# A smaller inverse for the first two steps, a's products on GpSimd, and a rewritten order in a chunked recurrence with soft routing

## The chip, the cores and the metric

One core of a Trainium2 chip. The time is device microseconds of one execution; the median of three runs of the kernel before is 380.5 us.

## The reference

For each of 4 batches and 8 heads (32 pairs) a 40x40 state runs over 768 steps of time. At each step the output row is `r_t @ state`, and then

```
Sa    = state @ a_t
state = state * w_t - outer(Sa, b_t) + outer(v_t, k_t)
```

The 32 outputs are joined into x, 3072 rows of 320. A soft mixture of 8 experts follows: `logits = x @ phi` (32 slots), a softmax over the rows sends rows to slots, each expert (320 to 1024, relu, back to 320) works on its 4 slots, and a softmax over the slots brings the results back to the 3072 rows.

## The kernel before, in words

**Chunks.** Time is cut into 12 steps (`st`, NST) of C = 64 positions, each of two halves (`q`) of 32; two steps make a super-step (`ss`). Inside a half the recurrence is a triangular system: with L the strictly lower part of b's products with a, u = (1 + L)^-1 g has to be found for each of the 32 pairs.

**Preparation of a step**, on data alone: `scan_s`, `scan_k` and `scan_c` (lines 758 to 807) make the running products of w by scans on VectorE (DVE), multiply k and b by one of them and a by the other; `bda_at` spreads a into a block-diagonal tile with ScalarE (ACT); `gram` and `lgram` multiply them on TensorE (PE) and mask them with DVE; `kbtok` and `ctok_of` transpose them. From step 2 on the scans stand in PSUM, in two halves of six groups.

**The solver** (lines 905 to 922) inverts the 32x32 triangles of a whole super-step at once: `solve_in` transposes on DVE and copies on ACT, then `solve_step(ss, i)` for i = 1 to 30 issues two instructions on GpSimd (POOL), a product of i x (31 - i) elements for each of 128 partitions and its addition, each needing the one before it; `solve_out` transposes back on DVE.

**The chain** of a step: `chain_g(st, q)` gathers g with products of the state and v, `chain_u(st, q)` (line 955) multiplies it by the inverse with 32 small products and copies it out negated, for q = 0 and then 1; `chain_s` (line 974) makes the next state. `y_vut`, `y_sd`, `y_p`, `y_y` compute the outputs of the step before; `slots_*` collect the routing every second step. Step st of the chain runs beside the preparation of steps st + 3 and st + 4, the outputs of step st - 1 and half of a later super-step's solver (`sol`, lines 1296 to 1303).

**The tail** (lines 1317 to 1405): the last outputs and the routing, the first expert layer, then for each half of the 320 output columns (`hf`) 64 products of the second layer into `so`, a sum, and 24 products of 160 columns that are copied out of PSUM two at a time and stored in runs given by `OX`.

**What sets the order.** Every call on `nc` is recorded by `Plan.record` (line 236) as an operation; successive products of one shape into one bank are joined into one. `Plan.schedule` (line 375) reads the order in which operations are placed from the string `ORDER`, two characters an operation; `forward` (line 383) estimates times, chooses PSUM banks, keeps POOL and DVE operations apart where both read SBUF (`clash`), and lets DMA issues on SyncE (SP) wait for PE work (`LAG`, `SLOTS`). `fill` puts products that compute nothing into estimated gaps of PE. All engines therefore run a fixed sequence each:

```
self.order = [self.ops[at[2 * i] * len(CODE) + at[2 * i + 1]] for i in range(len(self.ops))]
```

Of the kernel before, what the change touches and what calls it, by code (L numbers as in the profile page):

```python
# [116 lines left out]
class Engine:  # L117
# [35 lines left out]
    r"$w&/%f%g&<&=&?&@&A&B&(&R&S&T&U&[&]&`%{&a&e&f&g&h&k&l&9&s&t&u&v&w&x&y%)%s':%Z'3&8&z&{&|'$'%'i&O'j'q'r's&3't'u'v'w'x"
    r"(#'''+%~($%|(%',(&%[&2('(($,(.&0&K&:&1&5&*&J(/%]&4&;&+&,&p%^%b&%&-%a&m&F$-%h(6(7&$&q%z'&&)'1%i&>%3%j&E%k'2&&%l'/%m"
    r"%K&r%V$p&N'*&G&n%W%q%L%M%4&}'>&'%X'0&D%J%N'#$q'(&H&I&L&C&~(8&o'-%Y(Z%d%t%x%w'?%u%-%v'F%.'='`%e&6'@(c&7&V(9'B&X&Y&Z"
    r"'A'{'_&W&^'.';(<(0&i&c&_&j(1'4'|'9'<&d'C'}&M'a'D'U'6'5'G'7(2'H'I'J'K'Z']'X(='b'L'8(U'O'E'~'P'^'R(q'S(R(3'Y'Q'T'M(@"
    r"'c'd'f(j'e'V'y'W(4(S)&'N'[()(-(,(>([(?'g(A'z'm'k(+(5'n(*'l(B'o(G(Q(T(V(k'p(r(L(H(`(W(J(P(I(e(l)'(s(z({(C(d(O(|).(D"
    r'(i(K)0(E(a(M(b(g)*(y)((N(})1)/)+)])^+)+*+1)_+2+3+4+5+6+7+8+<+=+>+?+@+A+B+C+F+G+L+M))+N+O+P+Q+R+S+T+U+V+W+X+Y+`+a+h'
    r"+i+j+k+p+q+r+s+v+w(f)V(Y(v)z(X&Q);'h(:)@(w(t(;):)A)h(u(x%p),(o+x)=)2(^(m(h)-)3)B+y)<(F)C(p(~+z(n)>(_)4+{)i)|)R)S)H"
    r"(])?*.)P)T)5)D)j)Q)I)#)8)6)$)7)m)9)E)X)L)U*$){*'+|*6)Y)n)J)F)M)r)K*/*<*P*7)s+})%)G)e)`)k)f)c)d)Z)N*))a)b*2*%*3*H*8"  # L160
    r'*+)g)O*,*=*9)o***1)l*>*-,$*a*V*?)p*Q)[)t)W*E)q)u)w)v,%,&)y*z*W*@)~,O*L*y*4)x*^*F*[*i*R*A*]+I*B*#*_*&*:*C*M*`*N*S*h'
    r"*;*w+e*0*I*j)},@+H*k*O+K*x,'*b*J*(*c*o##,(+J*p+b*g*f+c+f%o+++~*d*e,G+%+E,3+g+&*D*K*T*5*U+d+#+$*q,>+,,R+(*r+-*s,P,^"
    r"-w+',W,C+.,#*u*t,k,l*v,X+Z+[,o+],Q,A,m,E+t+^,)+D,?+_+/-3+0,=+u-4,-,n*X,L,4,.,I*Y,p,U,_,a,`,B,5,/-Q,6,M,J,S,N,b,u,w"
    r',T,K,y,<,x,s,7,v,j,f,D-g,z,H,t,*-I-J,+,q.s-C-F.t.{.|.}.~/#/$/%/&-(/*-R-:/+/,,F/-/.///0/1/4/5/:/;/</=/>/?/@/A/B/C/D'
    r"/E/F/G-K/M,r,{%n,c,V/N/U/V/W/X-+,d-E-9-5-'-G-6-H-,-T/^,,/_/`/a/d/e/f,g,h,e,i,|,Y-Y,[,}.#-S,]0>-1-2.$-/,Z-0-D-<---Z"
    r'-*,~-=-;-.-i-U-?-@->.9-x-A/g-%-&-#-W-V-d.5-_-$-r-f-X.:*l-z-B-~.;.<*G-)/O.e-`-m*m-o-p/h-e.d/i-s/j-7/k/n-8-n*Z*n*{.%'
    r'.2-L-y.)-{-h-l-M-P.3.1.A.8*|-O/o.C+l-N-t.B-[-u/p*}-v-]/P.D-a.&*~.*.,.+.-.6.7-^-b-c.J-|.H.U.=+m...p./.o.K.L+n.>-k/Q'
    r'.?.@-j.0.I.f/R+9.T-}00.M.g.N.O.[+:.^.Q.P-q.R.`/q.u.S/r.m.n._.a.q.v0.,0/S/7,1.].V/H.w0E.W.y.x0B/60O/206.z.r/s.E/J/l'
    r"0L0-/K/I/L/t/80,/~03.'.b/90+/T.c0P/u0b0T.F+o/m+;0X/v0c180#.(0D19012b2c2j2k1f2l2m2n2o2p2q2u2v2w2x2y2z2{2|3#3$3)3*3+"
    r'3,3-3.3/30313233343536,83<3=3D3E3F0/0s0U0r0M020N0$0V090A0%0;/w/b07/33G3L0&3M3N3O3R0W/x0C0<0f0t0:3S0g0h0i0z0=0Y0@0x'  # L170
    r'/y0v/c0?3T0y0^0_0Q0w1$0`0R0j0u0S1%0|1H3U040a0d05120{0Z3V1#0}0[1C0]0~0k1(1X1D1Z0e.X.41U0l1).G1I.Y1+0m.Z1w0o1*3W100p'
    r".h0n1.1,0q1t1x1@1/.i1&1A083X3Y3]111'150H1g141l1Y1T0I.j1M1-/Y1_1S.k0J1F3^17161W1]1G0K/Z1R1;2'1?1=1<1|1V1>/[1E.l201N"
    r"210F1i1J1`/'1r2(3_1B0G1K1h1a22131L2)1c/(1d1O3`1s1^2R1b2$232%241u1e3%1:1P2*2&2C3&1j1Q2S1v2}2,2-2D1y1z251{2N2E2.2+1k"
    r"29273'3(2/3a2O3b2L2F3A2>2:2M282A2^2@2B1p3>1}3B2?1[2<1~/]3?2=3C,2/{2T2[2_2#/z3w2U3z2]44/|3x262`2h2i3v373c3:5=573~4@"
    r"4<3;384A4o1n392G1o0'2H4p5|3d5}6(6)6*3@6+6,6-6.6/636465666768696:6=6>6?6@6A6B6C6D6E6F6G6H6I6J6K6L2P6R6S6T1m6U6V3o3{"
    r'1q3}2;/)2a2~6W754*3p6]3f2I2J4+4,2d3y4%0(3|2K3g3h4&2f6^4=3q6_472e6`4P4>2Q6c452V2g4Q4?464$2W494:4F4D6d3e4R2X3P4S,92Y'
    r"4H6e6f4'6g6h4X4;4#482Z4V4K3Q4Y4-4B4W4L5B4I2r4G4Z4E3j4J5D4O4T4c4N5,4M4e4U4l6i745(5.5/4]4f4i5*3H4C4d3m4[4y5'5+5E3I4k"
    r'4^4j4r3n4s4m3J2s4v4n7<5)4g4t4w4u6j6k6l7=4{424h545$4x5R6m4_4.5A4|4}555%5&5c565U504z4/525J6;4~5S0)5Z5T5O4q535#4`5P5K'
    r"5V434a5Q4b3K4(5L4)5j5e5^5k6<6n5W5i5g5o5f5h5[5C5`5q5z5-7&5?,:5{3i6o5]5l/}7(5H5a5_7'5d5@5M6p3k5u5I5v5w5x6q5N6X6Y5X2t"
    r',;407)6M415m5b5y6P6N6Q5p5n51597D6Z6O5s7B5t7+6{7A5r7@5Y6|717*6}6t727.7J6&7k6u5>7/6$5~6v6#7C7-737P7N7F7G7S6%7,7a7K7I'  # L180
    r"7Q7H7L6r3Z6s7E7T7U7O7?7Z7X7R6a77703[7Y0*7]7_7W7M5:7g7{8,6'8&7e7^8$7b7z877:6x8%7l7}7|7V9)7c7h62607~8#3r587d8/7`3l6["
    r"7m7i7n7o7q7p8'808)7j7[8*7f8-7w888D7x8.7y6~7t848+7r618?8A857u7v818E8@868283988C8:7s6b8{8(7>8|8K5F8T3s8B8;898<8=8L8F"
    r'8z8`8N8H7#767$8J8a8I8^8G9<8R8U7%8P8_5;8[91938>9%789&6w7;8S8]8g8M968Q8h3t3u8i9?5G8k8j8V94959=6y8~8l8b9C8W8}8X8Y9D8O'
    r"9#8Z9'9E8m9A9>9$8n9I5<8p8d9(9F9h90979B8e998o8v9@9X9J9G9O8c9S8q9T8w9K9Q9^9`9R9Y9_9b9P9a9c9f9d8x9q799e9U9L9k9{9V6z9M"
    r'9Z9r9x8y:N9N9s9[9W9y9z9|9t9]9}8f9-9i8s9~9:9+9u:#9/:$9v:+:%9m8r8u:&9n9l:1:,:-:3:2:.:59g8t:/:0:4:7:8:692:I:9:::;9o9w'
    r":':<:=9p:?:>:A9,:@:B:O9H:_9j:P:C:`:Q:a:D:R9.:S:E:(:U:X:h:T:V:Y:F:]:i:G:b:W:^:c:):J:[:K:m:Z:M:j:l:k:d:g:e:f9;;7;8:*"
    r":L:H:n9*;9:r;:;;:s:o:p;C:t;D:q;A;R;B:u;E;P:v;>;H;Q;-;S;T;F;U;V:y;0:~;W;G;I;&;.;?;#;';J;1:w;+;$:x:{;%;<:|;K;(;=;X;4"
    r';);5;@;M;2;*;Y:z;3:};L;Z;N;,;/;6;O'
# [1280 lines left out]
```

## Time and profile before

| | |
|---|---|
| median of three runs | 380.5 us (379.73 to 381.6) |
| the profiled execution's own time | 377.92 us |
| its span, first to last instruction | 376.1 us |
| mean granted clock of TensorE | 0.941 |
| busy in the span: PE, DVE, POOL, ACT | 90%, 71%, 52%, 44% |
| moved by DMA | 63.05 MB, 168 GB/s on average |

All operations are issued from one place, so the profile gives them one line, L1223; the products that compute nothing have L479, and a stretch counted for L1223 alone leaves them out. Operations are told apart by engine, shape and tile: `wt` stands for the eight large tiles, in which most buffers lie, `mem`, `old` and `mid` for others, `ps` for the banks of PSUM, `cs_t` for the constants. A product in fp32 is seen as two records, each with a weight load (PEld). [...]

### The profile page before, as it was taken

The numbers are of one execution on the slowest core, as the hardware profiler recorded it, in microseconds if no ns is written. First come the engines' busy times: TensorE is split into PE (matmuls) and PEld (weight loads), VectorE is DVE, ScalarE is ACT, GpSimd is POOL, SyncE is SP. The second block draws the span as 40 slices with busy tenths as digits, with TensorE's granted clock in tenths as the row PEclk, the third lists the DMA queues.
The fourth block names the chain that finished last, engine by engine and source line by source line (L and its number), as shares of the span: only waits on it lengthen the run. The fifth ranks groups of instructions, "written<-read, shape, count | busy, mean of one in ns | idle before, by whom it ended". The sixth has DMA issues, their size and how long they took to land.

```text
span 376.1 us, 18254 instructions
## 1 busy us (share of the span) xinstructions
PE 337.4 (90%) x7957; PEld 291.6 (78%) x7957; DVE 267.0 (71%) x603; ACT 166.6 (44%) x377; POOL 195.0 (52%) x381
## 2 busy tenths in 40 slices
PE   8594888999999979899999998998999798999991
PEld 8592676888898969778898887998797687863791
DVE  5578896888989878878899797955476354573242
ACT  0543836535465452752745735352533223440331
POOL 3358888888688802888268870888600000020000
PEclk9966776999999998999999999999999889999996
DMA  7975674216645473433463535457486928799528
GB/s 190 244 185 142 163 184 131 68 34 159 160 134 170 122 172 88 132 86 82 104 192 93 163 83 170 141 151 215 119 240 189 290 74 250 199 345 416 205 99 321
DMA packets 35368, 63.05 MB, mean 168 GB/s; under 512 B 5001, under 2 KB 22521, under 8 KB 35289
## 3 DMA queue, kind: packets, MB, share of 16 engines
q1 hardware_dynamic: 35289, 61.89, 56.9%
...
q14 instruction: 17, 0.14, 0.1%
HBM read 57.94 MB, written 3.93 MB: 165 GB/s over the span
## 4 chain that ended last, share of the span: by engine, by line
PE 73%; DMA 7%; DVE 5%; ACT 5%; issue 4%; POOL 3%; SPq 1%; DVEq 0%; ACTq 0%
PE ps L1223 73%; DVE wt L1223 4%; ACT wt L1223 4%; POOL wt L1223 3%; DMA wt<-in_rr_dram 2%; DMA mem<-in_rr_dram 2%; DMA wt<-in_w_dram 1%; DMA wt<-in_kb_dram 1%; DMA wt<-in_ww_dram 1%; SPq L1223 1%; ACT L1223 0%; ACT mem L1223 0%; DVE mem L1223 0%; DVE ps L1223 0%; ACT ps L1223 0%
## 5 line engine op out<-in xcount | busy, mean ns | idle before, releaser
L1223 PE MATMUL ps<-wt,wt 128*64 128x40 f32 (+9 forms) x3432 | 144.0, 240 | 7.9 <-issue 6.2
L1223 PEld LDWEIGHTS ps<-wt,wt 120*32 120x32 f32 (+7 forms) x3432 | 128.3, 130 | 18.0 <-issue 10.9
L1223 POOL TENSOR_TENSOR wt<-wt 128x58 f32<-128x58 f32 (+14 forms) x180 | 90.3, 502 | 38.9 <-ACT wt L1223 25.3
L1223 POOL TENSOR_TENSOR wt<-wt,wt 128x58 f32<-128x58 f32 (+15 forms) x183 | 95.3, 521 | 27.7 <-ACT wt L1223 12.5
L1223 DVE TENSOR_TENSOR wt<-ps,cs_t 128x384 f32<-128x384 f32 (+6 forms) x132 | 62.8, 496 | 27.0 <-PE ps L1223 24.4
L1223 PE MATMUL ps<-cs_t,wt 120*128 120x120 f32 (+5 forms) x496 | 64.3, 267 | 8.7 <-DVE wt L1223 3.1
L1223 PE MATMUL ps<-wt,mem 120*64 120x192 f32 (+4 forms) x880 | 60.0, 311 | 8.2 <-ACT wt L1223 4.5
L1223 ACT COPY wt<-ps 128x320 f32<-128x320 f32 (+2 forms) x92 | 42.3, 474 | 51.8 <-PE ps L1223 42.8
L1223 PEld LDWEIGHTS ps<-cs_t,wt 120*128 120x128 f32 (+5 forms) x496 | 48.2, 144 | 19.0 <-ACT wt L1223 4.7
L1223 PEld LDWEIGHTS ps<-wt,mem 120*64 120x64 f32 (+4 forms) x880 | 47.5, 131 | 13.3 <-POOL mem L1223 4.7
L1223 ACT COPY mem<-ps 120x256 f32<-120x256 f32 (+6 forms) x99 | 37.4, 402 | 41.7 <-PE ps L1223 39.5
L1223 DVE TENSOR_TENSOR_SCAN ps<-ps,wt 120x390 f32<-120x390 f32 x40 | 38.6, 967 | 2.6 <-ACT old L1223 1.3
L1223 DVE TENSOR_SCALAR wt<-ps 32x320 f32<-32x320 f32 x48 | 23.7, 493 | 18.8 <-PE ps L1223 18.0
L1223 DVE TENSOR_TENSOR wt<-wt,ps 120x384 f32<-120x384 f32 (+1 forms) x80 | 34.1, 447 | 2.5 <-DMA wt<-in_kb_dram 2.0
L1223 POOL MEMSET mem<- 128x2048 f32 x1 | 1.8, 1807 | 62.2 <-PE ps L1223 62.2
L1223 PE MATMUL ps<-mem 32*32 32x40 f32 (+2 forms) x776 | 32.2, 224 | 0.8 <-DMA mem<-in_rr_dram 0.8
L1223 ACT ACTIVATE wt<-wt,bm_t 120x768 f32<-120x768 f32 (+1 forms) x36 | 30.0, 863 | 2.7 <-PE ps L1223 2.6
L1223 ACT ACTIVATE wt<-ps 32x320 f32<-32x320 f32 x48 | 20.5, 426 | 21.9 <-PE ps L1223 20.3
L1223 DVE STREAM_TRANSPOSE wt<-wt 128x1024 f32<-128x1024 f32 x12 | 25.1, 2095 | 0.2
L1223 PEld LDWEIGHTS ps<-mem 32*32 32x32 f32 (+2 forms) x776 | 19.8, 117 | 5.1 <-issue 1.2
L1223 DVE TENSOR_TENSOR ps<-ps,wt 120x480 f32<-120x480 f32 (+1 forms) x30 | 17.5, 600 | 6.7 <-PE ps L1223 6.5
L1223 PE MATMUL ps<-wt 32*32 32x40 f32 x1536 | 19.3, 199 | 2.7 <-issue 2.2
...
## 6 DMA issues: line engine op xcount, KB each, us to landing
...
wt<-in_rr_dram SPq DMA_DIRECT2D x96, 40.0 KB
...
```

Of the source, the lines that this page charges most:

```text
L1223: nc.vector.memset(ex, 0.0)
```

## The change

Five things, and a new `ORDER` for the 2222 operations that there are then (2240 before):

- The solver of super-step 0 inverts only the two 16x16 diagonal blocks of each triangle: 14 steps in place of 30, each over both blocks (`halves`). `lgram` of steps 0 and 1 writes the diagonal blocks and, with a second mask, the off-diagonal block (`nn`). `chain_u` of steps 0 and 1 multiplies g by the block inverse, copies (ACT), multiplies by the off-diagonal block, adds to g (DVE), and then goes on as before.
- From step 4 on a's product is one GpSimd instruction of 768 elements on the copy `cp`, in place of two on DVE; for steps 2 and 3 it stays on DVE.
- In the scans of steps 2 to 11, w is copied into both PSUM tiles, the scan runs in place and gives the whole product at once, so that the small product for `pc` becomes a copy on ACT; k's and b's product is issued once for each half of the groups in place of twice.
- Loads of w1 for the two large row blocks are split in two by columns, 32 in place of 16.
- In the tail the second layer's products are recorded in four parts for each half, and results leave PSUM three at a time; the second half is stored in five runs in place of seven.

```diff
-KV = 3
-BM, AV = NST, 2
-OX = ((6, 12, 18, 24), (4, 8, 12, 16, 20, 22, 24))
+PA = 4
+BM = NST
+OX = ((6, 12, 18, 24), (6, 12, 18, 21, 24))
...
 ORDER = (
...
-    cs_t = cst.tile([128, 451], F32, name="cs_t")
+    cs_t = cst.tile([128, 515], F32, name="cs_t")
+    mask_d, mask_n = cs_t[:, 451:483], cs_t[:, 483:515]
...
-                nc.sync.dma_start(wv[:, 2 * p + k], w1[2 * i + p, 128 * k:128 * k + 128])
+                for f in (0, 512):
+                    nc.sync.dma_start(wv[:, 2 * p + k, f:f + 512], w1[2 * i + p, 128 * k:128 * k + 128, f:f + 512])
...
+        nn, ys = cht(mid[:, 4 * HD:4 * HD + 1024]), mid[:, 0:HD]
...
         def scan_s(st):
-            if st > 1:
-                w_t, pc = raws[st], pcs.put(st)
-                sbk[st] = [[bank(f"s{k}{st}{x}")[0:120, 0:6 * CP + 2] for k in "kc"] for x in range(2)]
-                for x, (t, u) in enumerate(sbk[st]):
-                    a, g = 6 * CP * x, slice(6 * x, 6 * x + 6)
-                    t = t[:, 0:6 * CP]
-                    nc.scalar.copy(u, w_t[:, a:a + 6 * CP + 2])
-                    nc.vector.tensor_tensor_scan(
-                        t[:, ::-1], u[:, 2:6 * CP + 2][:, ::-1], one_f[:, a:a + 6 * CP][:, ::-1], 0.0, ALU.mult, ALU.add)
-                    nc.vector.tensor_tensor(pc[:, g], gcp(w_t[:, 0:NG * CP])[:, g, 1], gcp(t)[:, :, 0], ALU.mult)
-                    nc.vector.reciprocal(gcp(inj_f[:, a:a + 6 * CP])[:, :, 0], pc[:, g])
+            w_t, pc = raws[st], pcs.put(st)
...
+            sbk[st] = [[bank(f"s{k}{st}{x}")[0:120, 0:6 * CP] for k in "kc"] for x in range(2)]
+            for x, (t, u) in enumerate(sbk[st]):
+                a, g = 6 * CP * x, slice(6 * x, 6 * x + 6)
+                nc.scalar.copy(t, w_t[:, a + 1:a + 6 * CP + 1])
+                nc.vector.tensor_tensor_scan(
+                    t[:, ::-1], t[:, ::-1], one_f[:, a:a + 6 * CP][:, ::-1], 0.0, ALU.mult, ALU.add)
+                nc.vector.reciprocal(gcp(inj_f[:, a:a + 6 * CP])[:, :, 0], gcp(t)[:, :, 0])
+                nc.scalar.copy(pc[:, g], gcp(t)[:, :, 0])
+                nc.scalar.copy(u, w_t[:, a:a + 6 * CP])
         def scan_k(st):
-            if st > 1:
-                k_t = kbt(st)
-                for x, (t, _) in enumerate(sbk[st]):
-                    g, s_v = slice(6 * x, 6 * x + 6), gcp(t[:, 0:6 * CP])[:, :, 0:C].rearrange("p g (q t) -> p g q t", q=2)
-                    for q in range(2):
-                        nc.vector.tensor_tensor(k_t[:, g, :, q], k_t[:, g, :, q], s_v[:, :, q].unsqueeze(2).broadcast_to([120, 6, 2, 32]), ALU.mult)
+            k_t = kbt(st)
...
+            for x, (t, _) in enumerate(sbk[st]):
+                g = slice(6 * x, 6 * x + 6)
+                kv = k_t[:, g].rearrange("p g k q t -> p g k (q t)")
+                nc.vector.tensor_tensor(kv, kv, gcp(t)[:, :, 1:CP].unsqueeze(2).broadcast_to([120, 6, 2, C]), ALU.mult)
         def scan_c(st):
-            ah = ahs[st]
-            if st > 1:
-                cp = gc(cps.put(st))
-                for x in range(2):
-                    a, g, t = 6 * CP * x, slice(6 * x, 6 * x + 6), sbk[st][x][1][:, 0:6 * CP]
-                    nc.vector.tensor_tensor_scan(t, t, inj_f[:, a:a + 6 * CP], 0.0, ALU.mult, ALU.add)
+            ah, cp = ahs[st], gc(cps.put(st))
...
+            for x, (_, t) in enumerate(sbk[st]):
+                a, g = 6 * CP * x, slice(6 * x, 6 * x + 6)
+                nc.vector.tensor_tensor_scan(t, t, inj_f[:, a:a + 6 * CP], 0.0, ALU.mult, ALU.add)
+                nc.scalar.copy(cp[:, g], gcp(t)[:, :, 0:C])
+                if st < PA:
-                    nc.scalar.copy(cp[:, g], gcp(t)[:, :, 0:C])
-                return
...
+            if st >= PA:
+                nc.gpsimd.tensor_tensor(ah, ah, cp, ALU.mult)
         def bd_load(key, bd, src):
...
-                nc.vector.tensor_tensor(
-                    lls[ss][:, 2 * p:2 * p + 2].rearrange("p q h t -> p (q h) t"),
-                    lps[st].rearrange("p (x t) -> p x t", t=32),
-                    mask_l.unsqueeze(1).broadcast_to([128, 16, 32]), ALU.mult)
+                for t, mask in ((lls[ss], mask_d if ss == 0 else mask_l), (nn, mask_n))[:2 if ss == 0 else 1]:
+                    nc.vector.tensor_tensor(
+                        t[:, 2 * p:2 * p + 2].rearrange("p q h t -> p (q h) t"),
+                        lps[st].rearrange("p (x t) -> p x t", t=32),
+                        mask.unsqueeze(1).broadcast_to([128, 16, 32]), ALU.mult)
         def solve_in(ss):
...
+        def halves(t, r, c, m):
+            ap = [list(t.ap[0]), [528, 2], [32 if r is None else 0, c[1] if r is not None else c[0]], [1 if c[2] else 0, m]]
+            return bass.AP(tensor=t.tensor, offset=t.offset + (0 if r is None else 32 * r) + c[3], ap=ap)
         def solve_step(ss, i):
+            if ss == 0:
+                m = 15 - i
+                tv = tmp_r[i % 4][:, 0:2 * i * m].rearrange("p (k j t) -> p k j t", k=2, j=i)
+                nc.gpsimd.tensor_tensor(tv, halves(n_t, None, (i, 0, 0, i), m), halves(lt, i, (0, i, 1, i + 1), m), ALU.mult)
+                nv = halves(n_t, None, (i, 0, 1, i + 1), m)
+                nc.gpsimd.tensor_tensor(nv, nv, tv, ALU.add)
+                return
...
         def chain_u(st, q):
+            if st < 2:
+                for x, (l, r_) in enumerate(((tt, gs), (nn, ys))):
+                    yp = bank(f"y{x}s{st}")
+                    for h in range(H):
+                        for b in range(B):
+                            r = slice(32 * b, 32 * b + 32)
+                            nc.tensor.matmul(yp[r, h * D:(h + 1) * D], l[r, c, h, :], r_[r, h * D:(h + 1) * D], start=True, stop=True)
+                    if x == 0:
+                        nc.scalar.copy(ys, yp[:, 0:HD])
+                    else:
+                        nc.vector.tensor_tensor(gs, yp[:, 0:HD], gs, ALU.add)
...
         def solve_items(ss):
-                    + [lambda i=i: solve_step(ss, i) for i in range(1, 31)] + [lambda: solve_out(ss)])
+                    + [lambda i=i: solve_step(ss, i) for i in range(1, 31 if ss else 15)] + [lambda: solve_out(ss)])
         def y_lists(st, w):
...
+            nc.tag = x // 4
+        nc.tag = ""
...
-        for r in range(0, 24, 2):
+        for r in range(0, 24, 3):
-            for x in range(2):
+            for x in range(3):
-            (nc.vector.tensor_copy if r % 4 else nc.scalar.copy)(wts[hf][:, HC * r:HC * r + 2 * HC], op[:, 0:2 * HC])
-            if r + 2 in OX[hf]:
-                nc.sync.dma_start(out[hf, :, HC * at:HC * (r + 2)], wts[hf][:, HC * at:HC * (r + 2)])
-                at = r + 2
+            (nc.vector.tensor_copy if r % 2 else nc.scalar.copy)(wts[hf][:, HC * r:HC * r + 3 * HC], op[:, 0:3 * HC])
+            if r + 3 in OX[hf]:
+                nc.sync.dma_start(out[hf, :, HC * at:HC * (r + 3)], wts[hf][:, HC * at:HC * (r + 3)])
+                at = r + 3
...
+    dg = np.kron(np.eye(2, dtype=f4), np.ones((16, 16), f4))
-                             np.concatenate([st] * 4)],
+                             np.concatenate([st] * 4), -np.tile(st * dg, (4, 1)), -np.tile(st * (1 - dg), (4, 1))],
```

## Rows read from the trace of the kernel before

**Rows 1.** The page, busy time, share of the span and instructions of each engine

```profile
PE 337.4 (90%) x7957; PEld 291.6 (78%) x7957; DVE 267.0 (71%) x603; ACT 166.6 (44%) x377; POOL 195.0 (52%) x381
```

**Rows 2.** Timeline of POOL: start, length, merged instructions, wait ahead and its releaser

```profile
26.14 33.65 POOL L1223 TENSOR_TENSOR wt<-wt,wt 128x30 f32<-128x30 f32 x57 [1.89 <-ACT wt L1223]
...
60.80 30.43 POOL L1223 TENSOR_TENSOR wt<-wt 128x30 f32<-128x30 f32 x50
...
147.15 19.98 POOL L1223 TENSOR_TENSOR wt<-wt 128x30 f32<-128x30 f32 x34 [14.74 <-ACT wt L1223]
```

**Rows 3.** Timeline around the first product with the first inverse

```profile
62.14 0.55 DVE L1223 TENSOR_TENSOR wt<-ps,cs_t 96x384 f32<-96x384 f32 x1 [2.92 <-PE ps L1223]
...
63.08 2.00 DVE L1223 STREAM_TRANSPOSE wt<-wt 128x1024 f32<-128x1024 f32 x1
...
65.13 0.79 PE L1223 MATMUL ps<-wt 32*32 32x40 f32 x64
...
66.07 1.00 DVE L1223 TENSOR_SCALAR wt<-ps 32x320 f32<-32x320 f32 x2 [0.42 <-PE ps L1223]
```

**Rows 4.** Stretches: length, PE, PEld, DVE, ACT, POOL busy, clock, DMA share, GB/s

```profile
40.00:65.10 25.10, 19.48 (x312) 15.96 (x311) 20.24 (x42) 14.03 (x28) 21.73 (x47) 0.76 0.59 160
...
52.00:62.00 10.00, 9.13 (x59) 7.45 (x60) 6.60 (x17) 4.04 (x10) 8.51 (x23) 0.50 0.51 142
...
65.10:340.30 275.20, 261.00 (x6905) 228.90 (x6905) 208.27 (x475) 128.33 (x300) 150.43 (x300) 0.98 0.55 155
...
368.00:376.10 8.10, 0.00 (x0) 0.00 (x0) 1.48 (x4) 0.75 (x2) 0.00 (x0) 0.58 0.82 320
```

**Rows 5.** The same shape on PE at two clocks, timeline

```profile
59.53 1.59 PE L1223 MATMUL ps<-wt,wt 120*96 120x96 f32 x8
...
79.83 0.92 PE L1223 MATMUL ps<-wt,wt 120*96 120x96 f32 x8
```

**Rows 6.** Groups by shape, POOL: busy us, mean ns, idle ahead

```profile
L1223 POOL TENSOR_TENSOR wt<-wt,wt 128x30 f32<-128x30 f32 x12 | 3.0, 247 | 13.1 <-ACT wt L1223 12.5
...
L1223 POOL TENSOR_TENSOR wt<-wt,wt 128x240 f32<-128x240 f32 x12 | 7.7, 645 | 0.9
...
L1223 POOL TENSOR_TENSOR wt<-wt,wt 120x768 f32<-120x768 f32 x3 | 5.1, 1699 | 1.7 <-DMA wt<-in_aa_dram 1.7
```

**Rows 7.** Groups by shape, PE, ACT and DVE

```profile
L1223 PE MATMUL ps<-wt 32*32 32x40 f32 x1536 | 19.3, 199 | 2.7 <-issue 2.2 <-ACT wt L1223 0.5
...
L1223 ACT COPY wt<-ps 128x320 f32<-128x320 f32 x48 | 19.9, 428 | 39.5 <-PE ps L1223 38.2 <-issue 1.2
...
L1223 DVE SCALAR_TENSOR_TENSOR slx<-slx,mem,ps 128x320 f32<-128x320 f32 x5 | 2.7, 541 | 1.5 <-PE ps L1223 1.5
...
L1223 DVE TENSOR_TENSOR wt<-ps,cs_t 128x512 f32<-128x512 f32 x12 | 8.3, 688 | 3.6 <-PE ps L1223 3.6
...
L1223 DVE TENSOR_TENSOR wt<-wt,ps 120x384 f32<-120x384 f32 x60 | 31.5, 543 | 2.2 <-DMA wt<-in_kb_dram 2.0
...
L1223 ACT COPY ps<-wt 120x392 f32<-120x392 f32 x20 | 9.8, 491 | 6.6 <-DMA wt<-in_ww_dram 4.3 <-DVE wt L1223 2.2
```

**Rows 8.** Waits of the DMA queue on SP: us in total, times, longest

```profile
SPq L1223 <- PE ps L1223: 198.1, 129, 8.9
```

**Rows 9.** Timeline of the last 25 us

```profile
356.83 4.55 PE L1223 MATMUL ps<-wt,mem 128*32 128x160 f32 x126 [0.38 <-DMA wt<-in_w_dram]
...
363.31 8.68 SPq L1223 DMA_DIRECT2D out_dram<-wt  x11
...
367.40 2.08 DVE L1223 COPY wt<-ps 128x320 f32<-128x320 f32 x5 [0.79 <-PE ps L1223]
```

**Rows 10.** Timeline where the second inverse is done and first used

```profile
94.38 2.09 DVE L1223 STREAM_TRANSPOSE wt<-wt 128x1024 f32<-128x1024 f32 x1
...
103.17 0.79 PE L1223 MATMUL ps<-wt 32*32 32x40 f32 x64
```

More of the change, by code (lines that the diff above doesn't have):

```diff
@@ L153 @@
[L153 to L162, printed above, removed]
@@ L740, in rwkv_softmoe @@
         s0_t = kbks.tiles[3][0:120, 0:NG * CP]
-        scans = Ring([(kbks.tiles[2][0:120, 0:NG * CP], inj_f)])
+        s1_t = kbks.tiles[2][0:120, 0:NG * CP]
         bbs = [t.rearrange("p (g q t) -> p g q t", q=2, t=32) for t in (so_f[:, 2 * NG * C:3 * NG * C], rts.tiles[0].rearrange("p g c -> p (g c)"))]
@@ L772, in scan_s @@
-            w_t, s_t = raws[st], s0_t if st == 0 else scans.put(st)[0]
-            nc.vector.tensor_tensor_scan(
-                s_t[:, ::-1], w_t[:, 2:NG * CP + 2][:, ::-1], one_f[:, ::-1], 0.0, ALU.mult, ALU.add)
-            pc = pcs.put(st)
-            nc.vector.tensor_tensor(pc, gcp(w_t[:, 0:NG * CP])[:, :, 1], gcp(s_t)[:, :, 0], ALU.mult)
-            nc.vector.reciprocal(gcp(inj_f)[:, :, 0], pc)
-        def scan_k(st):
-            if st > 1:
-                k_t = kbt(st)
-                for x, (t, _) in enumerate(sbk[st]):
-                    g, s_v = slice(6 * x, 6 * x + 6), gcp(t[:, 0:6 * CP])[:, :, 0:C].rearrange("p g (q t) -> p g q t", q=2)
-                    for q in range(2):
-                        nc.vector.tensor_tensor(k_t[:, g, :, q], k_t[:, g, :, q], s_v[:, :, q].unsqueeze(2).broadcast_to([120, 6, 2, 32]), ALU.mult)
-                return
-            k_t, s_t = kbt(st), s0_t if st == 0 else scans[st][0]
-            for q in range(2):
-                eng = nc.vector if st < KV and q == 0 else nc.gpsimd
-                eng.tensor_tensor(
-                    k_t[:, :, :, q], k_t[:, :, :, q],
-                    gcp(s_t)[:, :, 32 * q:32 * q + 32].unsqueeze(2).broadcast_to([120, NG, 2, 32]), ALU.mult)
@@ new lines, in scan_k @@
+        def scan_k(st):
+            k_t = kbt(st)
+            if st < 2:
+                for q in range(2):
+                    eng = nc.vector if q == 0 else nc.gpsimd
+                    s_v = gcp((s0_t, s1_t)[st])[:, :, 32 * q + 1:32 * q + 33]
+                    eng.tensor_tensor(k_t[:, :, :, q], k_t[:, :, :, q], s_v.unsqueeze(2).broadcast_to([120, NG, 2, 32]), ALU.mult)
+                return
+            for x, (t, _) in enumerate(sbk[st]):
+                g = slice(6 * x, 6 * x + 6)
+                kv = k_t[:, g].rearrange("p g k q t -> p g k (q t)")
+                nc.vector.tensor_tensor(kv, kv, gcp(t)[:, :, 1:CP].unsqueeze(2).broadcast_to([120, 6, 2, C]), ALU.mult)
@@ new lines, in scan_c @@
+        def scan_c(st):
+            ah, cp = ahs[st], gc(cps.put(st))
+            if st < 2:
+                ct = raws[st][:, 0:NG * CP]
+                nc.vector.tensor_tensor_scan(ct, ct, inj_f, 0.0, ALU.mult, ALU.add)
+                nc.vector.tensor_tensor(ah, ah, gcp(ct)[:, :, 0:C], ALU.mult)
+                nc.scalar.copy(cp, gcp(ct)[:, :, 0:C])
+                return
[4 more added lines that the diff above has]
+                if st < PA:
+                    nc.vector.tensor_tensor(ah[:, g], ah[:, g], gcp(t)[:, :, 0:C], ALU.mult)
+            if st >= PA:
+                nc.gpsimd.tensor_tensor(ah, ah, cp, ALU.mult)
```

86 lines of the change are left out of this document (50 added, 36 removed).

## The prediction

> **What bounds the kernel now.** The page comes first: TensorE is busy for 337.4 us of 376.1, no other engine for more than 71% [rows 1]. That is a mean, so the stretches come next, without the products that compute nothing. From 65.1 to 340.3 us PE has 261.0 us of work in 275.2, with the clock at 0.98: 14.2 us are idle, in many small pieces, and DVE with 208.3 is second [rows 4]. There a chain that comes earlier gains only where PE has gaps. From 40.0 to 65.1 it is another kernel: PE has work for 19.5 of 25.1 us at a mean clock of 0.76, and POOL is the engine that is nearly full, 21.7 us. The timeline of POOL says why: the first solver runs from 26.14 without a break, 57 instructions to 59.8, its last three behind the start of the second solver, which goes on at 60.80 [rows 2]. Then the inverse is transposed at 63.08, 2.2 us late, because DVE had an operation in front that waited 2.92 us for PE, and the first `chain_u` starts at 65.13, 0.05 us after the transposition [rows 3]. So the start is bound by POOL's solver, and the rest by PE.
>
> **The solver.** By size an instruction goes from 0.247 us at 30 elements to 0.645 at 240, which is 0.190 us and 1.895 ns an element [rows 6]. Before: 60 instructions with 2 x 4960 elements, 11.4 + 18.8 = 30.2 us; from 26.14 to the last at about 60.8 it took 34.7, so 0.07 us lie between two. After: 28 instructions with 2 x 1120 elements, 5.3 + 4.2 + 28 x 0.07 = 11.5 us. The access runs over one more dimension; no row prices that, and between nothing and a tenth more I take nothing. The inverse is there at 37.6 in place of 60.8, 23.2 us earlier; with the transposition's 2.1 us, and no operation in front of it, `chain_u` can start at about 40, 25 us earlier.
>
> **The two sets more.** Four calls of `chain_u` (steps 0 and 1, two halves) get two sets of 32 products, 0.79 us a set (the shape takes 19.3 us for 24 sets) [rows 3, 7]: 8 x 0.79 = 6.3 us more PE work. On the chain each call gets 2 x 0.79, an ACT copy of 0.43, a DVE addition of 128x320 at 0.54 (nearest row, the one that also scales) [rows 7], and four handovers of 0.05 to 0.15 [rows 3]: 2.9 us, 11.7 in all. If nothing but the chain counted, 25 - 11.7 = 13.3 us would be left. Queued behind the wait for the copies are PE's products in its fixed order, so the order has to put other products there. The second mask for steps 0 and 1 is 2 x 0.69 on DVE [rows 7], and stands behind the solver's input, not in front.
>
> **What PE can take back.** The earlier chain must find room on PE. Between 40.0 and 65.1 there are 25.1 - 19.5 = 5.6 us of idle. From 52 to 62 the clock stands at 0.50, with 9.1 us busy [rows 4]; the same eight products take 1.59 us there and 0.92 at 79.83 [rows 5], so that at the full clock 9.1 would be 5.3, 3.8 less. A PE that is kept busy from 40 on can win 5.6 + 3.8 = 9.4, of which the new sets take 6.3: 3.1 are left. The ends are 13.3 (chain alone) and -6.3 (nothing won back); I take 3.1, as from 65.1 on PE is at 95% and whatever is brought forward was work to be done anyway.
>
> **a's products.** DVE loses 8 x 2 x 0.525 = 8.4 us (31.5 us for 60) [rows 7], POOL gets 8 x 1.70 = 13.6 [rows 6]. [...] But neither engine is the path: POOL works for 150.4 of the 275.2 us [rows 4], and the solver of a later super-step begins after a wait of 14.74 us for its input [rows 2]. Two products for each super-step, 3.4 us, are hidden in such gaps; without that cover they would delay an inverse by 3.4. I take 0 on POOL.
>
> **The scans.** ACT gets 20 copies more at 0.49, 9.8 us [rows 7], and 20 small ones that no row shows, between nothing and 0.43 each. It has 128.3 of 275.2 us busy, and the copies serve steps that are three or four ahead: 0; without that cover some 2 x 0.5 us stand ahead of a step's a product. DVE loses the small products and half the issues of k's products; less load there shortens waits of PE, and an order that keeps the gaps smaller can also avoid a clock drop like the one above. I take 1.5 of the 14.2 idle us back, between -2 (the new order meets other stalls) and 5.
>
> **Loads and tail.** The w1 split adds 16 issues, which at the 0.79 us an output issue takes (8.68 us for 11) [rows 9] is at most 12.6 us of SP's queue. SP waits 198.1 us for PE's pace [rows 8], so 0; uncovered, a late w1 piece would hold the first expert layer by one issue. The constants grow by 64 columns, 32 KB, 0.1 us at the 320 GB/s of the end [rows 4]. At the end, the first stored half of the output is held until the second layer's last products, 356.83 to 361.38; the stores are issued from 363.31, the last copy ends at 369.48, and the queues work on to about 375 [rows 4, 9]. The products in four parts let one half's results go out between the other half's products: 3.93 MB at 320 GB/s are 12.3 us, so stores from 357.5 could end at 370, 6 us earlier; PE's own work there stays the same, and the half that is last has to follow it by its copies and half of the bytes. Between 0 and 6 I take 2.
>
> **The sum.** 377.9 (the profiled execution's own time) - 3.1 - 1.5 - 2.0 = 371.3. The median of the runs stands 2.6 above that execution, so 374 is predicted for the median. A measurement of this kernel can tell about 0.5% from no change, 378.6 to 382.4.
>
> **Rivals.**
> *The chain passes in full.* If PE's busy time has slack inside, the whole 13.3 us comes through, with the other terms 380.5 - 13.3 - 3.5 = 363.7, 364. For it speaks that weight loads are busy for 78% only, against 90% [rows 1]; against it, that a set of 64 records takes 0.79 us wherever it stands [rows 3, 10]. [...] Chance 0.17.
> *DVE takes the place of POOL.* From 40.0 to 65.1 DVE is busy for 20.2 of 25.1 us [rows 4]. The free 4.9 lose 1.4 + 4 x 0.54 = 3.5 to the new masks and additions, so only 1.4 us of the chain's own work can come forward, and preparation is pushed back as far as the chain comes earlier. Then 6.3 are paid, 1.4 + 3.5 won: 381.9, no change. Chance 0.14.
> *The second inverse is late: slower.* Step 2 can't start without it. Before, the second solver started at 60.80, its result was transposed at 94.38, and step 2 took it at 103.17 [rows 2, 10]. With two a products in between it now needs 34.7 + 3.4 + 2.1 = 40.2 us from its start, and step 2 is due at 103.2 - 3.1 = 100.1, so it decides if it starts after 60. It can, if the chain's DVE work goes ahead of the preparation of step 3, whose b products it inverts. A start at 70 costs 10 us of a waiting PE: 384. For it speaks DVE's load above; against it, that POOL is now free from 37.6 on, so the order has 22 us to spare for it. Chance 0.11.
>
> **How the numbers follow.** The forecast has 0.58; its own range is 369 to 378.5 from the tail's and the scans' ends. The likeliest time is 374. The range goes down to 364 for the first rival and up to 382 for the second; the third and the ends of the tails beyond are left out. Faster by over 0.5%: 0.58 + 0.17 = 0.75; no change 0.14; slower 0.11.
>
> **What would show it.** Right: POOL's first solver with 28 instructions in some 11.5 us; a first `chain_u` near 40 with sets of 0.79 between copies; the next stretches with PE above 90% and the clock at 1.00 before 60; stores that start before the second layer's last products are done. The forecast is wrong if step 2's first use of its inverse (103.17) comes over 8 us earlier (first rival), less than 1 us earlier or later (second), or right behind a transposition that ends after 101 (third).

## The result and the profile after

The changed kernel is slower: 383.4 us (median of 20) against 378.3 for the kernel before, a ratio of 1.013 with a 95% interval of 1.009 to 1.017, where 374.0 and a gain had been predicted. Executions of one kernel differ: the twenty of the kernel before run from 373.2 to 389.9 us, and compared with itself in the same way it gave 0.989 (0.979 to 0.998). A difference of 1% between two comparisons of a few executions proves little here, and the 0.5% of the prediction was too fine a measure. Medians below are over all executions of a comparison, while ratios with an interval leave out executions over 1.5% above the quickest of their kernel, so that the two need not agree.

The page of the changed kernel, from an execution of 383.19 us (span 381.4), engines and the two instruction queues [rows 1]:

```profile
PE 345.6 (91%) x8507; PEld 295.9 (78%) x8507; DVE 261.0 (68%) x547; ACT 177.5 (47%) x419; POOL 188.3 (49%) x357
...
q8 instruction: 67, 1.10, 1.2%
q14 instruction: 16, 0.13, 0.1%
```

Timeline of POOL, the first solver and the start of the second [rows 2]; it holds the 28 instructions forecast:

```profile
28.52 8.66 POOL L724 TENSOR_TENSOR wt<-wt,wt 128x28 f32<-128x28 f32 x20 [3.54 <-ACT wt L724]
37.24 0.15 POOL L724 MEMSET wt<- 128x32 f32 x1
37.32 2.96 POOL L724 TENSOR_TENSOR wt<-wt,wt 128x88 f32<-128x88 f32 x8
49.54 0.55 POOL L724 TENSOR_TENSOR wt<-wt 128x30 f32<-128x30 f32 x2 [9.26 <-ACT wt L724]
```

The solver takes 11.8 us and is done at 40.28. But the timelines of DVE and PE show the transposition of the inverse at 51.76 and the first extra set at 53.93 [rows 3]; the set on `mid` is the second, 57.05 is u, and 105.46 is step 2's first use of its own inverse [rows 10]:

```profile
46.31 2.07 DVE L724 STREAM_TRANSPOSE wt<-wt 128x1024 f32<-128x1024 f32 x1
...
49.39 0.98 DVE L724 TENSOR_TENSOR_SCAN ps<-ps,wt 120x390 f32<-120x390 f32 x1
...
51.76 2.02 DVE L724 STREAM_TRANSPOSE wt<-wt 128x1024 f32<-128x1024 f32 x1
...
53.93 0.78 PE L724 MATMUL ps<-wt 32*32 32x40 f32 x64 [0.19 <-DVE wt L724]
55.61 0.79 PE L724 MATMUL ps<-mid 32*32 32x40 f32 x64
57.05 0.91 PE L724 MATMUL ps<-wt 32*32 32x40 f32 x64
...
105.46 0.79 PE L724 MATMUL ps<-wt 32*32 32x40 f32 x64
```

The stretches say why the inverse lies for 11 us: DVE is busy for 23.8 of the 24 us from 32 to 56 (columns as in [rows 4]; here and below the products that compute nothing are counted too):

```profile
32.00:40.00 8.00, 6.63 (x126) 5.36 (x125) 8.00 (x17) 6.52 (x14) 6.63 (x19) 1.00 0.71 187
40.00:48.00 8.00, 7.14 (x157) 5.58 (x156) 8.00 (x12) 5.78 (x15) 0.26 (x1) 1.00 0.56 154
48.00:56.00 8.00, 6.73 (x182) 5.84 (x186) 7.80 (x16) 4.89 (x11) 5.37 (x15) 1.00 0.76 199
56.00:64.00 8.00, 6.22 (x260) 5.23 (x246) 3.67 (x9) 5.57 (x14) 7.37 (x11) 1.00 0.30 78
```

In three more traces of this kernel the inverse lies for 12.9 to 14.2 us. The clock, the share of full speed that TensorE is granted, is not always at 1.00 there; the third of these stretches in an execution of 389.94 us:

```profile
48.00:56.00 8.00, 7.75 (x67) 6.84 (x68) 7.07 (x15) 3.89 (x9) 6.03 (x16) 0.50 0.57 136
```

From the first product with the inverse to step 2's first use of its own, first in the changed kernel, then in the kernel before, where PE has next to no idle time:

```profile
53.90:105.40 51.50, 46.07 (x1550) 39.42 (x1550) 35.15 (x68) 23.57 (x56) 33.29 (x63) 1.00 0.36 95
```

```profile
65.10:103.10 38.00, 36.90 (x1071) 32.76 (x1070) 33.93 (x68) 18.46 (x41) 31.23 (x65) 1.00 0.40 108
```

Cut at step 2's first use and at the first use of an inverse by the last step, the executions fall into three stretches; first the changed kernel's middle and end, then the kernel before's:

```profile
105.40:313.60 208.20, 197.89 (x5284) 175.44 (x5282) 153.71 (x316) 101.96 (x245) 127.76 (x241) 0.98 0.51 141
313.60:381.40 67.80, 58.06 (x1047) 42.26 (x1045) 29.00 (x98) 22.80 (x59) 3.18 (x5) 0.96 0.79 273
```

```profile
103.10:310.10 207.00, 196.42 (x5235) 173.72 (x5231) 156.52 (x349) 97.49 (x224) 116.03 (x231) 0.98 0.52 146
310.10:376.10 66.00, 54.92 (x1035) 42.07 (x1033) 27.98 (x98) 21.65 (x59) 3.17 (x5) 0.95 0.76 262
```

So in this pair of traces the changed kernel loses 2.3 us before step 2 (the chain starts 11.2 earlier and takes 51.5 us in place of 38.0), 1.2 in the middle and 1.8 at the end. One pair is thin ground. In a second trace of each (spans 381.5 and 374.6) step 2 comes at 106.21 and 101.44, the middle is 206.0 and 203.3, the end 69.3 and 69.9: 4.8 are lost before step 2, 2.7 in the middle, nothing at the end. The start loses most in both. Last, the largest entry of PE's waits from 16 to 345 us, for the changed kernel, and for the kernel before, where it is second:

```profile
PE ps L724 <- issue: 11.4, 14, 2.3
```

```profile
PE ps L1223 <- issue: 9.2, 11, 2.1
```

"issue" is idle time of PE for which the profile shows nothing that was waited for. The prediction has no term for it.

### The profile page after: what moved, and what is told of

Its sections match the earlier page's. It is cut to its first block, busy times and chain, and to the rows that moved or that the text cites. A ratio compares the mean times of both kernels' runs of the same rounds, so it can differ in the third digit from the quotient of the medians.

```text
span 388.1 us, 19346 instructions
## 1 busy us (share of the span) xinstructions
PE 355.0 (91%) x8507; PEld 306.0 (79%) x8507; DVE 261.3 (67%) x547; ACT 177.3 (46%) x419; POOL 188.5 (49%) x357
## 4 chain that ended last, share of the span: by engine, by line
PE 79%; DMA 7%; DVE 7%; issue 5%; ACT 1%; SPq 0%; ACTq 0%; DVEq 0%
PE ps L724 79%; DVE wt L724 5%; DMA wt<-in_w_dram 2%; DMA wt<-in_kb_dram 2%; DMA wt<-in_ww_dram 1%; DMA wt<-in_rr_dram 1%; ACT wt L724 1%; DVE ps L724 0%; SPq L724 0%; DVE mem L724 0%; DVE old L724 0%; PE ps L480 0%; DVE mid L724 0%; DVE slx L724 0%; ACT ps L724 0%
## 5 line engine op out<-in xcount | busy, mean ns | idle before, releaser
L724 PE MATMUL ps<-wt,wt 128*64 128x40 f32 (+9 forms) x3432 | 146.2, 239 | 5.2 <-issue 2.9
L724 PEld LDWEIGHTS ps<-wt,wt 120*32 120x32 f32 (+7 forms) x3432 | 130.6, 130 | 17.1 <-issue 7.2
L724 POOL TENSOR_TENSOR wt<-wt 128x238 f32<-128x238 f32 (+15 forms) x184 | 97.1, 529 | 44.2 <-ACT wt L724 30.8
L724 POOL TENSOR_TENSOR wt<-wt,wt 128x238 f32<-128x238 f32 (+20 forms) x155 | 82.0, 530 | 49.2 <-ACT wt L724 23.3
L724 ACT COPY wt<-ps 128x320 f32<-128x320 f32 (+3 forms) x108 | 44.0, 430 | 55.5 <-PE ps L724 31.0
L724 PE MATMUL ps<-wt,mem 120*64 120x192 f32 (+4 forms) x880 | 62.1, 310 | 7.1 <-POOL mem L724 2.7
L724 ACT COPY mem<-ps 120x480 f32<-120x480 f32 (+6 forms) x99 | 37.7, 402 | 44.1 <-PE ps L724 38.4
L724 PE MATMUL ps<-wt 32*32 32x40 f32 x1792 | 24.1, 202 | 5.4 <-issue 4.2
L724 DVE TENSOR_TENSOR wt<-ps,wt 120x480 f32<-120x480 f32 (+2 forms) x37 | 21.1, 584 | 11.3 <-PE ps L724 5.5
L724 PEld LDWEIGHTS ps<-wt 32*32 32x32 f32 x1792 | 19.9, 108 | 10.7 <-issue 6.1
```

The source lines that it names most:

```text
L724: eng.dma_start(dst, src)
```

## The experiments

**The changed kernel again, and the extra sets.** The first kernel is the changed one; the second has the sets, copies and additions removed, the third keeps them but takes their waits away. All three keep its order.

```diff
 # without sets
-            if st < 2:
-                for x, (l, r_) in enumerate(((tt, gs), (nn, ys))):
...
 # sets off the chain
-                for x, (l, r_) in enumerate(((tt, gs), (nn, ys))):
+                for x, (l, r_) in enumerate(((tt, gs), (nn, gs))):
...
-                        nc.vector.tensor_tensor(gs, yp[:, 0:HD], gs, ALU.add)
+                        nc.vector.tensor_tensor(ys, yp[:, 0:HD], ys, ALU.add)
```

> The changed kernel itself, once more. Three theories for its loss of some 5 us. CHAIN: the two extra sets a call put copies, additions and waits on the chain of steps 0 and 1, while the first inverse is transposed only at 51.4 us, because VectorE's fixed order has other work in front; the chain's start gains 8.8 us and then loses 13.6. WORK: the loss is the 6.3 us of extra TensorE products, wherever they stand. LOADS: the loss is born at the end, where TensorE waits for w1 and w2. CHAIN and WORK expect step 2's first use of its inverse at 106 to 108 us (103.2 before) and a lag of 4 to 5 us from there on that the end only keeps; LOADS expects the lag to be under 2 us at 300 us and to come after it. All expect 379 to 384 us.

> The changed kernel without the two extra sets a call, their copies and additions; everything else stays in the same order. It leaves out the products that complete the inverse, so the first two steps use block inverses alone. CHAIN expects 8 to 12 us less than the changed kernel (some 371 to 375), with step 2's first use some 10 us earlier; WORK expects 6 us less (some 376); LOADS expects at most 1 us less.

> The changed kernel with all its products, copies and additions in the same order, but the second set takes the same operand as the first and its sum goes to a scratch tile: TensorE has the same work and no product waits for a copy or an addition any more. The correction of the inverse is left out of the result. CHAIN expects the waits to go: 4 to 6 us less than the changed kernel. WORK and LOADS expect no change (within 1 us).

Measured beside each other: before 378.8 us, changed 382.6, without sets 375.2, off the chain 378.6 (372.6 to 385.5). The sets cost 7.3 us, the waits perhaps 3.9 of them. Timeline of PE and instruction queue without the sets:

```profile
96.77 0.79 PE L723 MATMUL ps<-wt 32*32 32x40 f32 x64
...
q8 instruction: 63, 1.03, 1.2%
```

Step 2's use is 8.7 us earlier and so is the end (9.6 in the span). From the first product with the inverse to step 2 it now takes 40.1 us:

```profile
56.60:96.70 40.10, 38.48 (x1040) 33.47 (x1038) 31.13 (x57) 20.74 (x50) 29.08 (x55) 1.00 0.40 110
```

But even with the early inverse and no sets the kernel is only 3.5 us below the one before, of which two of seven executions took 369.3 and 370.0.

**The end of the kernel.** Four more: w1's loads whole again in the changed kernel; the kernel before itself; the same with its order fitted anew, as a control; and the kernel before with the change's tail, or with w1's split, alone. Fitting moves operations in `ORDER` so that the kernel's own estimate gets shorter.

```diff
 # w1 whole (the reverse for the split alone)
-                for f in (0, 512):
-                    nc.sync.dma_start(wv[:, 2 * p + k, f:f + 512], w1[2 * i + p, 128 * k:128 * k + 128, f:f + 512])
+                nc.sync.dma_start(wv[:, 2 * p + k], w1[2 * i + p, 128 * k:128 * k + 128])
 # tail alone
-        for r in range(0, 24, 2):
+        for r in range(0, 24, 3):
...
```

> The changed kernel with w1 loaded in whole pieces as before (16 load issues less), the order fitted anew to that. LOADS expects 3 to 6 us less than the changed kernel and shorter waits for w1 in the last 80 us; CHAIN and WORK expect no change (within 1.5 us).

> The kernel before itself, once more, to see where its quicker executions (369 to 370 us among the runs beside the last kernels) are quicker than its profiled one (377.9). CHAIN expects the difference in the start, where the clock stood at half speed from 32 to 40 and from 52 to 62 us: step 2's first use of its inverse some 6 to 8 us earlier than 103.2, and the same distance from there to the end. LOADS expects it in the last 80 us.

> The kernel before with its order alone fitted anew, as a control for the next two kernels, which needed that: no theory expects a gain or a loss from it; within 3 us of the kernel before.

> The kernel before with the change's end alone (the second layer's products in four parts, three copies a bank, five stores for the second half), order fitted anew. The prediction's step expects 2 us less than the control. CHAIN expects 0 to 2 us less, since the loss lies in the first steps; LOADS expects 1 to 3 us more than the control.

> The kernel before with w1's loads in halves alone, order fitted anew. The prediction's step and CHAIN expect no change against the control (within 2 us); LOADS expects 3 to 6 us more.

Whole w1 gave 389.3, 6.8 more than the changed kernel beside it, the opposite of LOADS, though with a new order too. In the second group the kernel before had 380.0 (377.1 as a kernel of its own in the same comparison; its profiled span is 374.6 beside 376.1). The execution profiled there, 376.4, is not one of the quick ones, so what made those quick stays open. The control came to 381.5, a ratio of 1.016 (1.008 to 1.024): by the ratio a miss, as nothing but the order had changed; by the medians it is 1.5 above the one and 4.4 above the other. The tail alone had 382.8, ratio 1.014 (1.004 to 1.024), the split alone 386.3 (380.9 to 396.3), ratio 1.018 (1.006 to 1.030). Against the control neither ratio differs. The tail's 2 us are not seen, though intervals of 1% to either side could hide them. The split's median is 4.8 above the control, as LOADS expected, its ratio is not, so the split alone stays open. For the changed kernel LOADS fails by the stretches above: 3.5 of the 5.3 us are lost before the last step begins. A new order alone can cost as much as the whole loss to be explained; every kernel with a fitted order is read with that in mind.

**An earlier chain.** Only `ORDER` differs in the first kernel: step 4's four scans, 0.98 us each and among the work ahead of the transposition, stand behind the first chain call. But that order is fitted anew from start to end: at most 705 of its 2222 operations keep their order among each other, so what the control showed holds for this kernel as well. The second has the same order and no sets; the third has the full solver, no sets and an order of its own.

```diff
 # full solver (and the sets removed as above)
-                    + [lambda i=i: solve_step(ss, i) for i in range(1, 31 if ss else 15)] + [lambda: solve_out(ss)])
+                    + [lambda i=i: solve_step(ss, i) for i in range(1, 31)] + [lambda: solve_out(ss)])
```

> The changed kernel with another order and nothing else: the scans of step 4, which VectorE does before the first transposition although step 4 needs them only some 40 us later, and which hold four PSUM banks, stand behind the first chain call; the transposition of the first inverse follows the solver's end. All expect the first extra set near 46 instead of 54 to 56 us. CHAIN: the chain of the first steps is what sets the time, so step 2's first use of its inverse comes 4 to 6 us earlier than in the changed kernel and the end as much: 377 to 379. SECOND INVERSE (the prediction's third rival): step 2 then waits for the second inverse, which is no earlier: 0 to 2 us less, 381 to 383. WORK: no change.

> The early-chain kernel without the extra sets, their copies and additions (the products that complete the inverse are left out, as in the run without sets). CHAIN expects the sets to cost here too: 5 to 8 us less than the early-chain kernel. SECOND INVERSE expects the chain to be waiting for the second inverse by then, with or without sets: at most 2 us less, and step 2's first use at the same time in both. WORK expects 6 us less, all of it on TensorE.

> The change without its first part: the full solver for the first super-step and no extra sets, with the scans, a's products, w1's loads and the end of the changed kernel; the order fitted anew around the later inverse. The prediction's step (an early inverse is worth 9.4 us, the sets cost 6.3) makes it 3 us slower than the changed kernel, 385 to 386. CHAIN says that the early inverse is worth less than the sets cost: 2 to 5 us less than the changed kernel, 378 to 381. LOADS, with the losses in the other parts, expects it like the changed kernel.

> The changed kernel once more, beside the three others on the same chip: 381 to 384 us by all theories.

Measured: before 380.1, early chain 388.2 (ratio 1.024, 1.014 to 1.034), without sets 384.9, full solver 384.9, changed 386.7. PE in the early-chain kernel, timeline, then its middle and end:

```profile
46.77 0.79 PE L723 MATMUL ps<-wt 32*32 32x40 f32 x64
...
101.66 0.79 PE L723 MATMUL ps<-wt 32*32 32x40 f32 x64
```

```profile
101.60:309.90 208.30, 196.90 (x5286) 173.65 (x5283) 151.50 (x317) 102.78 (x249) 128.61 (x242) 0.99 0.50 141
309.90:382.10 72.20, 62.69 (x1046) 46.88 (x1045) 28.27 (x98) 22.27 (x58) 3.27 (x5) 0.89 0.74 258
```

The chain starts 7.2 us earlier, CHAIN got nearly its 4 to 6 us at step 2 (101.66 against 105.46), and the end did not move: the last stretch gave 4.4 back, with the clock at 0.89. No theory had expected 388. Without the sets, in the same order, step 2 stands at 100.92 and the median is 3.2 lower, between CHAIN's 5 to 8 and SECOND INVERSE's at most 2. Full solver and early inverse cannot be told apart, in the medians or at step 2 (106.47, against 105.46 and 106.21 in two traces of the changed kernel).

**Work without waits.** To separate the price of waits from that of work, masked products of the outputs are done twice in both kernels, 64 records away from the chain and 6.6 us of PE by an estimate from 0.87 us for eight of the largest; the sets off the chain are timed again.

```diff
-                for x in range(2):
+                for x in (0, 1) * (2 if 3 * st + u < 4 else 1):
                     for k in range(2):
                         nc.tensor.matmul(g[64 * k:64 * k + 64, 2 * w * x:2 * w * (x + 1)], vut[0:n, k, 2 * i + x],
```

> The changed kernel once more, as the measure for the kernels beside it on the same chip: 381 to 387 us by all theories.

> The kernel with the extra sets kept and their waits gone, once more with more rounds, since its first four times (372.6 to 385.5) left open what the waits cost. CHAIN: 4 to 6 us less than the changed kernel beside it; WORK: within 1 us of it; a value in between says that both count.

> The kernel before with work added to TensorE alone: the masked products of the first step's output and the first third of the second step's are done twice, 64 records of 120x192 and less, 6.6 us at 0.87 us for 8, in the same places of the same order (about 66 to 90 us), none of it on the chain of the first steps. WORK expects the whole 6.6 us in the time, as TensorE has no room from 65 us on: 384 to 386. CHAIN expects that step 2 waits for its chain and its inverse anyway and that the gaps there take half of it or more: 0 to 3 us more than the kernel before.

> The changed kernel with the same 6.6 us of TensorE work added in the same way (the same products done twice). Between 56 and 96 us its TensorE is idle for 4 to 6 us behind the chain's waits. WORK expects 6 to 7 us more than the changed kernel beside it; CHAIN expects the gaps to take part of it: 0 to 3 us more.

Measured: before 377.7, changed 387.7 (ratio 1.028, 1.018 to 1.039), sets off the chain 382.6 (1.017, 1.008 to 1.025), before with work 379.8 (1.006, 1.000 to 1.011), changed with work 380.2 (1.012, 1.005 to 1.019). The waits are worth 5 us this time by the medians. Where they stood the trace shows little of it, 50.3 us from the first set to step 2 after 51.5, though with the clock at 0.95:

```profile
56.00:106.30 50.30, 46.95 (x1546) 40.27 (x1544) 33.31 (x64) 23.54 (x56) 30.06 (x57) 0.95 0.35 97
```

The kernel before with 6.6 us of work more takes 2.1 more. But the changed kernel with more work is 7.5 us *faster*, which no theory allowed. Its PE lost less to "issue":

```profile
PE ps L723 <- issue: 5.2, 8, 1.2
PE ps L479 <- issue: 1.3, 1, 1.3
```

Its middle, and that of the kernel before with the same work, whose "issue" time did not fall:

```profile
110.20:309.40 199.20, 194.62 (x5285) 172.88 (x5284) 152.87 (x315) 101.42 (x245) 126.95 (x239) 1.00 0.54 146
```

```profile
PE ps L1221 <- issue: 9.5, 13, 1.7
...
105.10:308.80 203.70, 193.72 (x5234) 172.36 (x5230) 156.82 (x350) 97.37 (x224) 116.35 (x232) 0.99 0.52 148
```

**The place in the instruction stream.** A record is one entry of PE in the trace, two for a product in fp32. In the profiles of the changed kernel these gaps come at the same products each time, and from one to the next lie 127, 253, 381, 507 or more PE records, multiples of some 127. The added work, 64 records, had moved every later product by half of that. Two kernels do that alone, with tiny products at a time when PE waits for data:

```diff
         for _ in range(n):
+        if src is self.idle[0]:
+            for x in range(32):   # 64 in the second kernel
+                r = slice(32 * (x % 4), 32 * (x % 4) + 32)
+                self.nc.tensor.matmul(bank[r, 0:16], src[r, 0:32], src[r, 0:16], start=True, stop=True)
```

> The changed kernel with 32 small products that compute nothing (64 records, under 1 us) behind those at its start, where TensorE waits for data; all else, the order, the banks and the waits, stays. STREAM (the gaps of TensorE without a visible wait stand at every 127th record or a multiple, and what they cost depends on which products they fall on): the gaps come 64 records earlier in the work, their sum between 16 and 345 us changes by over 2 us from the 11.5 of the changed kernel, and the time with it, downwards if it is an unlucky layout: 378 to 382. CHAIN and WORK expect no change: within 1 us of the changed kernel, a ratio to the kernel before of 1.013 to 1.028.

> The same with 64 small products (128 records, under 1.5 us). STREAM expects the gaps back at the same products as in the changed kernel, one spacing later in the count, the same sum of 11 to 12 us and the same time as the changed kernel (ratio 1.013 to 1.028). CHAIN and WORK expect the same time too; a time as different from the changed kernel as that of the other shift says that the spacing is not what decides.

Measured: before 378.4, shifted by 64 records 376.9 (371.9 to 383.2), by 128 records 384.3 (381.2 to 386.8). Half a spacing takes 7.4 us off against a whole one, which has the changed kernel's ratio of the other comparisons (384.3 to 378.4, 1.015); the changed kernel itself was not beside them. PE's "issue" from 16 to 345 us in the one and the other, and the middle and end of the first:

```profile
PE ps L728 <- issue: 6.4, 10, 1.7
```

```profile
PE ps L728 <- issue: 9.6, 11, 2.5
...
PE ps L484 <- issue: 0.8, 1, 0.8
```

```profile
110.30:310.60 200.30, 195.46 (x5284) 173.63 (x5282) 153.26 (x317) 101.76 (x245) 128.43 (x242) 1.00 0.54 146
310.60:375.90 65.30, 55.88 (x1046) 41.73 (x1045) 28.96 (x98) 22.78 (x59) 3.18 (x5) 0.99 0.82 283
```

The middle has the same 5284 records as in the changed kernel and is 7.9 us shorter, and the kernel with work added agrees (199.2). Only there is something gained: step 2 itself comes 4.9 later than in the changed kernel's trace. One gap of the changed kernel shows how: timeline of PE, then stretches of 3 us, then the instruction queue in the DMA view of 254.25 to 254.50 us:

```profile
254.57 0.33 PE L724 MATMUL ps<-mem 80*64 80x80 f32 x2
257.21 0.40 PE L724 MATMUL ps<-mem 80*64 80x80 f32 x1 [2.31 <-issue]
```

```profile
252.00:255.00 3.00, 2.90 (x134) 2.47 (x119) 1.59 (x7) 1.47 (x4) 2.61 (x6) 1.00 0.90 203
255.00:258.00 3.00, 0.79 (x10) 0.77 (x10) 0.34 (x1) 0.13 (x1) 2.69 (x5) 0.69 0.85 243
258.00:261.00 3.00, 3.00 (x17) 2.95 (x16) 0.70 (x3) 1.34 (x4) 2.69 (x5) 0.50 0.15 54
261.00:264.00 3.00, 3.00 (x23) 2.80 (x23) 1.82 (x4) 0.00 (x0) 2.68 (x5) 0.67 0.05 14
264.00:267.00 3.00, 3.00 (x53) 2.61 (x53) 2.09 (x6) 1.57 (x6) 2.61 (x5) 1.00 0.36 124
```

```profile
q8 instruction: 1, 0.02, 33.3%
```

PE stands still between two products of one form; a packet of instructions starts to move at 254.45, the end of that view, and PE goes on at 257.21, 2.8 us later. The other four gaps between 260 and 302 us (271.35, 281.49, 297.00, 301.12) end 2.4 to 2.6 us after the start of such a packet. So it is throughout: of the 15 gaps called "issue" in this trace, the 14 above and one ahead of a product that computes nothing, all end 2.2 to 3.0 us after a packet's start, of the 21 gaps with a visible wait 6 do. Then the clock is at 0.50 and rises again between 261 and 264: the 3 us at 0.50 alone lose 1.5 us of full speed, and the stretches before and after it some of theirs, so that a gap of 2.3 us costs nearer to twice that, an estimate. It need not: in a second execution the same gap, 2.16 us up to 257.43, leaves the clock at 1.00, and PE gets through 31 records in place of 17:

```profile
258.00:261.00 3.00, 3.00 (x31) 2.87 (x32) 1.99 (x5) 1.34 (x4) 2.69 (x5) 1.00 0.25 88
```

67 packets of 1.10 MB are 16.4 KB each, and the kernel without sets, with 512 records less by its edit, has 4 packets less (63): one packet for 128 records; PE's 8507 records over the 67 packets are 127 for each. That the gaps are late packets is inferred from count, place, time and the two shifts; what sets the time at which a packet is fetched is open.

## Why the prediction was wrong

**The solver** was right: 11.8 us for 11.5.

**"With no operation in front of it, `chain_u` can start at about 40"** is the first step that failed. The inverse was there at 40.28, but DVE, busy for 23.8 of 24 us, reached its transposition at 51.76; 11 of the 25 us came through. The prediction counted DVE's load in 40.0 to 65.1 only for its second rival, and there as a sum. The row of an operation ahead of the transposition [rows 3] had already said that DVE's order, not only POOL's solver, stood there. [Rows 10] was also misread: 94.38 is the input of the third solver; the second inverse's transposition stood at 98.72.

**The extra sets** were sized well, 0.79 us each; the chain grew by 13.5 us, and is 11.4 shorter in the run without them, where 11.7 had been worked out. But the room that had been counted for them, 9.4 us of idle time and half clock, lay ahead of the chain: in the stretch that they lengthen PE was already busy for 36.9 of 38.0 us. Without them the time falls by 7.3 us; without their waits by 3.9 and 5.1 in two comparisons, and where in the execution these are won is not shown. PE work away from the chain costs part of its length: 2.1 us for 6.6 in the kernel before, whose place in the stream it shifts too, and about 4 in the changed kernel against the shifted one, whose products are moved by the same 64 records (medians of 380.2 and 376.9, which are 1.007 and 0.996 of the medians of the kernel before beside them).

**"A PE that is kept busy from 40 on can win 9.4"** is the second. PE was not busy: in the four stretches above it idles 5.3 of 32 us (32 - 6.63 - 7.14 - 6.73 - 6.22) although the clock is at 1.00, first because DVE and ACT prepare, then behind the copies of the sets; and in the execution of 389.94 us the clock stands at 0.50 from 48 to 56, so that the 3.8 us of the clock were not safe either. That a PE kept busy keeps its clock, as this term and the scans' have it, the trace before shows only in part: at or shortly ahead of the falls to 0.50 at 31.4, 51.9, 140.7 and 297.7 us PE stands still for 1.26 to 2.35 us, but behind the 1.55 us up to 45.67 the clock stays at 1.00. The start, priced at -3.1, came out at +2.3 and +4.8 in two pairs of traces. Step 2 later than before is the sign that the prediction gave to its second rival, DVE in POOL's place (381.9); that the third's 384 lies nearer to 383.4 is luck, as is shown below.

**The scans' 1.5 and the tail's 2.0** are not seen: the middle is 1.2 us longer, the end 1.8, and the tail alone did no better than its control. The tail's sign did come, as the first store is issued ahead of the last products of the second layer, and brought no time:

```profile
366.10 11.04 SPq L724 DMA_DIRECT2D out_dram<-wt  x9
...
367.08 3.47 PE L724 MATMUL ps<-wt,mem 128*32 128x160 f32 x96
```

The scans were not run alone; the two changed kernels moved by 64 records have a shorter middle than the kernel before (199.2 and 200.3, against 203.3 to 207.0), and whether the scans have a part in that is open. **a's products** at nothing have nothing against them, though they too were not run alone: one takes 1.82 us, and the second inverse is done at 87.6 and transposed only at 102.34. That ends after 101, the third rival's sign, but PE works up to step 2 without waiting for it, so the rival did not come. **The w1 split** at nothing is open, as said above.

**What the sum did not have** is the place of products in the instruction stream. It is worth 7.4 us between two shifts of one kernel, more than the three terms of the sum together. With the better one the changed kernel has 376.9 beside 378.4, which cannot be told from no change. As far as the runs show, the loss measured is a start that lost where it should have gained, and a layout that is some 7 us worse than another one. The kernel before with work added is moved by 64 records too and gains nothing by it in its trace ("issue" 9.5 after 9.2, a middle of 203.7 against 207.0 and 203.3); other shifts of it were not tried. Its middle has 207.00 - 196.42 = 10.6 us of idle PE, like the changed kernel's 10.3, where the shifted one has 4.8. A kernel that beats both by more than the spread is not shown; the run without sets, 375.2, leaves out part of the computation.
